# Scoring two units of a quad in one visit, with a new bank map and new planner constants, in a fused attention and gated-MLP block

## The chip, the core and the metric

The kernel runs on one core of one Trainium2 chip. The metric is device time in microseconds (us), the median of several runs; lower is better. Five engines work side by side, each with its own queue in order: TensorE (PE in the profile), VectorE (DVE), ScalarE (ACT), GpSimd (POOL) and SyncE (SP), which here issues nearly all DMAs. Data lies in SBUF; TensorE writes its products to PSUM, which has 8 banks of 128 partitions x 512 f32.

## The reference

It is one transformer block with adaptive layernorm: 2048 tokens, width 640, 32 heads of 20, MLP width 1536, in bf16.

```python
mod = (silu(c) @ w_mod).reshape(1, 6, 1, 640)      # sa, ca, ga, sb, cb, gb
h = layernorm(x) * (1 + ca) + sa
qkv = (h @ wqkv)                                   # 3 x 32 heads x 20
p = softmax(q @ k.T * 20 ** -0.5)
x = x + ga * ((p @ v) @ wo)
h = layernorm(x) * (1 + cb) + sb
x = x + gb * (((h @ w_gate) * (h @ w_up)) @ w_down)
```

There are 32 x 2048 x 2048 scores, and each needs an exponential.

## The kernel before, in words

**A planner writes the program.** `build_kernel` runs on the host. It makes a `Task` for each piece of work (engine, estimated duration, what it depends on, priority) and steps a model clock (`Sched.run`): whenever an engine is free in the model, the ready task of best priority is put next in that engine's list. The five lists are then emitted as they are, with semaphore waits for the dependencies that cross engines (`emit_program`). On the chip every engine works through its list in order, so where a task takes longer than its estimate, what stands behind it waits. PE has its own choice of the next task in `pick_pe`.

**Tiling.** Queries go in five chunks (`CHUNKS`: 512, 512, 512, 256, 256). A chunk has eight items, each one set of four heads (`items`). An item's scores are cut into units of 128 keys x 512 queries (two key tiles x 256 queries in the short chunks), 64 units an item in the long chunks. The four heads of a set lie in four groups of 32 partitions, and products of different groups run on PE at once.

**Two ways to the exponential.** Most units are scored into a group's own PSUM banks, two units at a time (even groups hold three units from group `HEADG` on), and ACT takes the exponential of a whole group in one instruction (L1444), writing the bf16 tile PP. A part of the units goes to DVE instead. `QUADS` says how many quads (four units, one for each head) of each item. DVE adds a bias to the scores, clamps at 0 and converts to int16 (L1468, 128x512, into the tile DB); the result, read as bf16 bits, is a first estimate of the power of two. Two masks (L1500 keeps the mantissa, L1508 the exponent) and one product (L1505) over the whole quad, 128x2048, then give two terms in DSS whose sum is a quadratic estimate of the exponential. The value products (PV, L1970) sum over both terms. So a unit of a quad costs one DVE read, a quarter of three wide DVE instructions, and twice the PV products.

**PE's order.** `pick_pe` first looks whether the next group's scores can be issued (a score visit). Units of quads are attached to such a visit by `d_attach`, up to two in a visit, when they come due (`due`, from `D_LEAD`), when their keys and queries are there and when one of the shared PSUM banks `G` is free. Else it takes PV products, or a round of other products (projections, the suffix), or a fill product on the identity, which is issued where the activity of the last 3.4 us in the model falls under `FILL_MIN`.

**Banks.** Before, even groups use banks 0, 1 (and 2 from `HEADG` on), odd groups 3, 4; bank 7 is for PV; the shared slots `G` are 5, 6 and 2, of which 2 is given up at `HEADG`.

**End of an item.** DVE transposes the PV sums (T1, L1592) and takes the reciprocal of the denominators (L1599); POOL multiplies (OTn, L1600); DVE transposes back (L1607); SP issues four or five small DMAs that lay the heads into Ocp (L1619). After an item 7 all of a chunk's outputs are there.

**The suffix of a chunk** (`suffix`) runs while the next chunk's scores do: the product with wo, in two halves for each tile of 128 tokens, and the residual (L1690); batch-norm statistics (L1704, L1706); variance plus epsilon, and its power -0.5 on POOL (sd L1707, rs L1709); xn, which subtracts the mean and multiplies by rs (L1711); transposes of xn on PE (L1728) and their evacuation with scale and shift (h2T, L1733); gate and up products, `hprod`, the product with wd, and the output. In chunks 0 to 2 xn stands on POOL (`XN2_POOL = 3`, with an estimate of 760 ns); in chunks 3 and 4 it stands on DVE (estimate 360 ns). With `XN2_LK = 2` the planner lets an xn on POOL start only when no ready DVE task that is marked `lk` waits, and lets neither engine start a marked task while the other runs one. The weights of gate and up come in slices (stg, L1768) by SP.

The late projections of the queries (`LATEQ`, fourth quarter of the tokens) are written to a DRAM buffer q_rows (L1177) and read back in another layout (QT, L1199), all by SP. `LATEQ_A` and `LATEQ_F` say from which group on they may run.

**The tail** is the suffix of the last chunk, which has no scores beside it.

Of the kernel before, what the change touches and what calls it, by code (L numbers as in the profile page):

```python
# [12 lines left out]
SEM = 60.0  # L13
# [14 lines left out]
STEAL_END = 66197.894  # L28
STEAL_GAP = 187.231
HAM_W = 3413.3  # L30
# [290 lines left out]
def emit_program(nc, sched, nsem_dma=56):  # L321
# [83 lines left out]
    with nc.Block() as block:  # L405
# [20 lines left out]
        def _(e):  # L426
# [6 lines left out]
         (3, 4, 3, 4, 3, 3, 4, 4),  # L433
         (3, 3, 4, 3, 3, 4, 4, 4),
         (1, 2, 1, 2, 1, 1, 1, 2),
         (1, 1, 1, 1, 1, 1, 1, 1))
D_LEAD = 0.381
NB0, NSS = 2, 3
HEADG = 579
OP_EARLY = 0  # L440
EV_OP = 0.5
T_SPLIT = 1
GU_OUTER = 4
# [6 lines left out]
XBACK = 1  # L450
HOLD = 110
PVTOL = 253
XDPRIO = 3.0
TPRIO = 0.75
# [7 lines left out]
WM_GATE = 9  # L462
WM_NEED = 1.838
K_DIRECT = (0, 1, 2, 3)
Q_DIRECT = 2
K_LEAD = 0.755
K_ALL = (0,)
KD_LEAD = 0.212
DMA_WINDOW = 900000
D_LATE = 16  # L470
D_RES = 63
PVMIN, PVMAX, PVCAP = 2, 10, 12
PV0 = 0
# [11 lines left out]
PV0N = 1  # L485
XN2_LK = 2
XN2_POOL = 3
RC_POOL = 0
RC_COST = 900
GATE_F = (0.793, 0.688, 1.105, 0.744, 1.0)  # L490
FILL_MIN = 4156.882
FILL_HARD = 0.0
# [6 lines left out]
XFIRST = 0  # L499
LN2P = 2.344  # L500
NALT = 1
OPFIRST = 0
HT_L = 0.02
V_L = 0.246
LATE_A = 3.254
LATE_L = 1.2
LATEQ = (3,)
LATEQ_A = 2
LATEQ_F = 0.578
QUAD_GAIN = 0.597233983857778  # L510
NTERM = 2
XHALF = 1
X_LATE = -0.231
X_HALF = 0.0
# [10 lines left out]
def build_kernel(nc, A_x, A_wqkv, A_wo, B_x, B_w_gate, B_w_up, B_w_down, c, w_mod, out):  # L525
# [169 lines left out]

    G = Slots([5, 6, 2] if HEADG else [5, 6], "G")
    GX = Slots([3, 4] if HEADG else [2, 3, 4], "GX")
    hx = (1, 3) if HEADG else (1, 3, 4)
# [25 lines left out]
    def pool(dur, f, deps=(), prio=3.0, **k):  # L724
        t = Task("pool", dur, f, deps, prio=prio, **k)
        t.lk = 1
        return sc.add(t)
# [63 lines left out]
    def load_rest():  # L791
# [5 lines left out]
        for q, f in enumerate((first2[0], first2[1],  # L797
# [14 lines left out]
                                               fill=1.0, base=0, channel_multiplier=1), [p_i0], prio=0)  # L812
    p_mh = pool(100, lambda e: e.memset(mhalf[:, 0:2], -0.5), prio=1)
    p_m1 = pool(100, lambda e: e.memset(mhalf[:, 2:4], -1.0), prio=2)
    p_on = dve(600, lambda e: e.memset(Vf[:, :].rearrange("p (h w) -> p h w", w=VW)[:, :, 0:1], 1.0), prio=-1)
# [463 lines left out]
    while ap < NA:  # L1279
        even = len(glist) % 2 == 0  # L1280
        us = ubuf[ap:ap + (3 if even and len(glist) >= HEADG else 2)]
        apos.append(ap)
        ap += len(us)
        glist.append((us, 0 if even else 3))
    NG = len(glist)
# [176 lines left out]
    for qi, (it, us) in enumerate(dquads):  # L1462
        st_ = d_state[qi]
        for x, u in enumerate(us):
            cell = {}

            def fp1(e, st_=st_, x=x, cell=cell):
                return e.tensor_scalar(DB0[:, st_["slot"], x * 512:(x + 1) * 512], bank(cell["b"]), EBIAS, 0.0,  # L1468
                                       op0=ALU.add, op1=ALU.max)
            tp = Task("dve", ps_cost(512), fp1, [], prio=0.8, name=f"P1.{qi}.{x}")  # L1470
            tp.on_start = lambda task, cell=cell: G.done(cell["b"], task)
            u.task = (tp, cell)
            sc.left += 1
            st_["p1"][x] = tp
# [109 lines left out]
    def item_end_tasks(it):  # L1584
# [9 lines left out]
        item_info[it]["t1"] = t1  # L1594
        den = OT[:, 0:n].rearrange("p (b c) -> p b c", c=32)[:, :, 0:1]
        if RC_POOL and it < len(items) - 1:
            t2 = pool(RC_COST, lambda e: e.tensor_tensor(invT[:, 0:nb32].unsqueeze(2), den, mhalf[:, 2:3].unsqueeze(2).to_broadcast([128, nb32, 1]), ALU.pow), [t1, p_m1], prio=0)
        else:
            t2 = dve(155, lambda e: e.reciprocal(invT[:, 0:nb32].unsqueeze(2), den), [t1], prio=1.5)  # L1599
        f3 = lambda e: e.tensor_tensor(  # L1600
# [41 lines left out]
    def suffix(ci):  # L1642
# [31 lines left out]
        for tl in range(ntl):  # L1674
# [28 lines left out]
            for hf in range(2):  # L1703
# [6 lines left out]
                      [p1], prio=1)  # L1710
            fx2 = lambda e, t=t, tl=tl: e.tensor_scalar(  # L1711
                xn2[:, tl, :], xck[:, tl, :], mv2[:, t, 0:1], rs2[:, t:t + 1], op0=ALU.subtract, op1=ALU.mult)
            if XN2_POOL and ci < XN2_POOL:
                tx = pool(760, fx2, [p2] + first, prio=1)
                tx.lk = XN2_LK
            else:
                tx = dvl(360, fx2, [p2] + first, prio=LN2T if tail else LN2P)
            t_xn2.append(tx)
            x1_done += ev
# [407 lines left out]
    def d_attach(ts, t, pos, rows, limit, relax):  # L2127
        n = 0
        while n < limit:
# [18 lines left out]
            if dst["fresh"]:  # L2148
# [5 lines left out]
                dst["fresh"] = False  # L2154
            b, rel = G.take(ga[1], 1)
            tp, cell = pick.task
            cell["b"] = b
            ts.deps = ts.deps + unit_score_deps(pick) + rel
            ts.emits = ts.emits + unit_score_emits(pick, lambda b=b: bank(b))
            tp.deps = [ts] + st_["brel"]  # L2160
# [8 lines left out]
    def pick_pe(t):  # L2169
# [44 lines left out]
        elif not tail_added[0]:  # L2214
            tail_added[0] = True
            la = [a for a in act_tasks[-2:]]
            if all(a.done is not None for a in la):
                for b in range(5):
                    if b != 2 or not HEADG or back[0]:
                        G.add(b, la)  # L2220
            else:
                tail_added[0] = False
# [143 lines left out]
```

## Time and profile before

| what | us |
|---|---|
| median of three runs | 848.92 (848.4 to 850.7) |
| the profiled execution, its own time | 848.4 |
| its span, first to last instruction | 846.8 |
| first exponential starts | 16.2 |
| last exponential ends | about 813.4 |
| ACT idle in the span | 67.6 |
| DVE idle in the span | 120.9 |
| mean granted TensorE clock | 0.972 of full speed |

The profile shows one execution. A group's row gives line, engine, operation, tiles (out<-in), shape, count, then busy time and the mean of one, then how long the engine was idle just before these instructions and what ended that. Neighbouring instructions of one engine overlap a little, so the time from start to start is below the mean of one: 14 exponentials of 1024 columns that ran without a break took 13.07 us, 0.93 each, while their mean is 1.125. A timeline line of several instructions gives their start, the time from the first's start to the last's end, and in brackets the idle time before. PE's ends are modelled, so a busy PE need not be at its peak. The granted clock says how much of full speed TensorE was given.

### The profile page before, as it was taken

The page shows a single profiled execution, that of the slowest core. Times are in us where ns is not written, and L with a number is a line of the kernel's source. Part 1 is how long each engine was busy: PE and PEld are TensorE (multiplying, and loading weights), DVE is VectorE, ACT ScalarE, POOL GpSimd, SP SyncE. Part 2 cuts the span into 40 slices and gives each one's busy share as a digit, 9 for nine tenths or more (in the row PEclk, how much of TensorE's full clock was granted, in tenths as well). Part 3 has the DMA queues.
Part 4 walks back from the last instruction along what each step waited for, and adds up shares of the span by engine and source line. Part 5 has one row for each costly group of instructions (what it writes and reads, how often), then busy time and mean ns, then how long its engine had stood idle before and what let it go on. Part 6 is the DMA issues. An engine that isn't in the chain of part 4 may idle for free.

```text
span 846.8 us, 29000 instructions
## 1 busy us (share of the span) xinstructions
PE 804.5 (95%) x12557; PEld 310.2 (37%) x12557; DVE 725.9 (86%) x1260; ACT 779.2 (92%) x821; POOL 106.8 (13%) x118
## 2 busy tenths in 40 slices
PE   9999999999796999999999799999998999999998
PEld 4433233222231223323332222334343444554567
DVE  7898999999777699999999798998987877767773
ACT  7889999999887699999999699999998999999952
POOL 3300000010015000000005300000034000001000
PEclk9999999999989599999999799999997999999999
DMA  9724211114310025200210022100300136204520
GB/s 293 218 75 100 72 43 36 44 31 123 105 36 26 24 55 154 59 7 22 60 45 6 5 56 61 37 5 29 91 9 3 39 90 122 60 23 107 129 61 23
DMA packets 116445, 54.72 MB, mean 65 GB/s; under 512 B 83915, under 2 KB 116319, under 8 KB 116319
## 3 DMA queue, kind: packets, MB, share of 16 engines
q1 hardware_dynamic: 115391, 51.72, 23.9%
q8 instruction: 100, 1.64, 0.8%
q10 hardware_dynamic: 928, 1.15, 0.4%
q14 instruction: 26, 0.21, 0.1%
HBM read 41.85 MB, written 8.41 MB: 59 GB/s over the span
## 4 chain that ended last, share of the span: by engine, by line
ACT 37%; PE 33%; DVE 15%; issue 8%; POOL 5%; DMA 1%; SPq 0%; ACTq 0%; DVEq 0%; POOLq 0%
ACT PP L1444 37%; PE ps_all L1408 10%; PE ps_all L871 9%; PE ps_all L1970 7%; DVE DB L1468 6%; POOL xn L1711 4%; PE ps_all L867 3%; DVE DSS L1505 2%; DVE DSS L1508 2%; DVE DSS L1500 1%; PE ps_all L1131 1%; PE ps_all L1067 1%; PE ps_all L1728 1%; DMA wm<-in_w_mod_dram 1%; DVE OT L1592 1%
## 5 line engine op out<-in xcount | busy, mean ns | idle before, releaser
L1444 ACT ACTIVATE PP<-ps_all 128x1024 bf16<-128x1024 f32 (+1 forms) x777 | 760.2, 1178 | 33.5 <-PE ps_all L1408 31.4
L1408 PE MATMUL ps_all<-QT,KT 32*128 32x512 bf16 (+1 forms) x2560 | 314.6, 346 | 16.1 <-ACT PP L1444 12.1
L1468 DVE TENSOR_SCALAR DB<-ps_all 128x512 int16<-128x512 f32 x396 | 263.0, 681 | 50.6 <-PE ps_all L1408 49.3
L1408 PEld LDWEIGHTS ps_all<-QT,KT 32*128 32x128 bf16 x2560 | 82.2, 91 | 268.0 <-ACT PP L1444 232.5
L1970 PE MATMUL ps_all<-PP,Vf 128*32 128x512 bf16 (+2 forms) x2088 | 167.9, 349 | 0.3 <-DVE OT L1592 0.2
L871 PE MATMUL ps_all<-h2T,stg 128*32 128x512 bf16 (+1 forms) x1780 | 119.8, 347 | 1.1 <-DVE DB L1468 0.4
L1505 DVE TENSOR_TENSOR DSS<-DB,DSS 128x2048 bf16<-128x2048 bf16 x99 | 120.8, 1220 | 0.0
L1600 POOL TENSOR_TENSOR OTn<-OT,invT 128x512 bf16<-128x512 f32 (+1 forms) x39 | 42.8, 1096 | 600.0 <-DVE invT L1599 596.2
L1970 PEld LDWEIGHTS ps_all<-PP,Vf 128*32 128x32 bf16 (+1 forms) x2088 | 46.7, 94 | 91.9 <-issue 84.5
L1970 PE MATMUL ps_all<-DSS,Vf 128*32 128x512 bf16 (+3 forms) x944 | 78.9, 357 | 0.7 <-DVE DSS L1508 0.5
L1500 DVE TENSOR_SCALAR DSS<-DB 128x2048 int16<-128x2048 int16 x99 | 72.2, 730 | 1.0
L1508 DVE TENSOR_SCALAR DSS<-DB 128x2048 int16<-128x2048 int16 x99 | 69.3, 700 | 0.0
L871 PE MATMUL ps_all<-wd,hprod 128*32 128x320 bf16 (+1 forms) x1320 | 57.6, 283 | 1.1 <-DVE DB L1468 0.8
L871 PEld LDWEIGHTS ps_all<-h2T,stg 128*32 128x32 bf16 x1780 | 39.7, 96 | 36.7 <-issue 18.8
L871 PEld LDWEIGHTS ps_all<-wd,hprod 128*32 128x32 bf16 x1320 | 30.7, 96 | 18.1 <-issue 8.3
L1592 DVE STREAM_TRANSPOSE OT<-ps_all 128x512 f32<-128x512 f32 (+1 forms) x40 | 24.1, 603 | 13.6 <-PE ps_all L1970 13.5
L1711 POOL TENSOR_SCALAR xn<-xck,mv,rs 128x640 bf16<-128x640 bf16 x12 | 32.2, 2689 | 12.0 <-DVE DSS L1505 11.5
L871 PE MATMUL ps_all<-wo,Ocp 128*32 128x320 bf16 (+1 forms) x640 | 29.0, 291 | 4.1 <-DMA Ocp<-OcT 3.9
L1970 PEld LDWEIGHTS ps_all<-DSS,Vf 128*32 128x32 bf16 (+1 forms) x944 | 24.1, 96 | 22.4 <-issue 10.9
L1131 PE MATMUL ps_all<-hT,wq 128*32 128x512 bf16 x375 | 31.9, 382 | 0.0
L2290 PE MATMUL ps_all<-ident 128*32 128x512 bf16 x352 | 30.9, 386 | 0.4
L871 PE MATMUL ps_all<-wV,hT 128*32 128x320 bf16 (+1 forms) x688 | 31.1, 291 | 0.0
(123 smaller groups left out, 542.3 us busy)
## 6 DMA issues: line engine op xcount, KB each, us to landing
stg<-in_B_w_gate_dram SPq DMA_DIRECT2D x50, 160.0 KB
stg<-in_B_w_up_dram SPq DMA_DIRECT2D x50, 160.0 KB
QT<-q_rows SPq DMA_DIRECT2D x22, 128.0 KB
KT<-k_rows SPq DMA_DIRECT2D x84, 32.0 KB
wm<-in_w_mod_dram SPq DMA_DIRECT2D x3, 800.0 KB
x<-in_A_x_dram SPq DMA_DIRECT2D x7, 320.0 KB
xck<-in_A_x_dram SPq DMA_DIRECT2D x3, 640.0 KB
wd<-in_B_w_down_dram SPq DMA_DIRECT2D x1, 1920.0 KB
```

What stands on the lines that cost most here:

```text
L871: return lambda e, b: e.matmul(ps[32 * x:32 * x + 32, b, c0 + o:c0 + o + w], lhs()[:, 32 * x:32 * x + 32], rhs() if w == n else rhs()[:, o ...
L1131: f = [lambda e, b_, k=k, x=x: e.matmul(ps[x:x + min(32, w - x), b_, :], wx[:, k, r0 + x:r0 + min(x + 32, w)], hT[tc][:, k, :], tile_posit ...
L1408: ems.append(lambda e, i=i, kt=kt: e.matmul(dstf()[:, i * u.n:(i + 1) * u.n], KT[32 * u.s:32 * u.s + 32, u.j, kt * 128:(kt + 1) * 128], QT ...
L1444: return e.activation(PPs[g % 2][:, cellp["p"], 0:nu * 512], ps[:, b0:b0 + nu, :].rearrange("p b c -> p (b c)"), AFT.Exp, scale=ESCALE)
L1468: return e.tensor_scalar(DB0[:, st_["slot"], x * 512:(x + 1) * 512], bank(cell["b"]), EBIAS, 0.0, op0=ALU.add, op1=ALU.max)
L1500: return e.tensor_scalar(DSS[:, st_["ss"][0], :], DB0[:, st_["slot"], :], 0x7F, 0x3F00, op0=ALU.bitwise_and, op1=ALU.bitwise_or)
L1505: return e.tensor_tensor(d, DB0[:, st_["slot"], :].bitcast(BF16), d, ALU.mult)
L1508: return e.tensor_scalar(DSS[:, st_["ss"][1], :], DB0[:, st_["slot"], :], 0x7F80, 2, op0=ALU.bitwise_and, op1=ALU.bitwise_or)
L1592: t1 = Task("dve", n * 1.1 + 70, lambda e: e.transpose(OT[:, 0:n], ps[:, BPV, 0:n]), [], prio=0.0, name=f"T1.{it}")
L1600: f3 = lambda e: e.tensor_tensor(OTn[:, 0:n].rearrange("p (b c) -> p b c", c=32), OT[:, 0:n].rearrange("p (b c) -> p b c", c=32), invT[:, ...
L1711: fx2 = lambda e, t=t, tl=tl: e.tensor_scalar(xn2[:, tl, :], xck[:, tl, :], mv2[:, t, 0:1], rs2[:, t:t + 1], op0=ALU.subtract, op1=ALU.mult)
L1970: ems.append(lambda e, i=i, kt=kt, stt=stt, stp=stp: e.matmul(ps[32 * s:32 * s + mc, BPV, 0:u.n], Vf[:, (kt * H + 4 * u.j + s) * VW:(kt * ...
```

## The change

It does five things.

1. `xn` of chunks 0 to 2 goes back from POOL to DVE, as in chunks 3 and 4; the options for it, and the unused option to take the reciprocal on POOL, are removed.
2. Bank map: odd groups use banks 5, 6; the shared slots are 4, 3 and 2, so that two of them are neighbours (3 and 4, or 2 and 3).
3. Pairs: `d_attach` looks, for each unit that it attaches, for a second unit of the same quad that is also ready. Where banks 3 and 4 (or 2 and 3) are both free and the second unit is due as well, both are scored in this visit, and one DVE instruction of 128x1024 reads both banks and writes both places of DB. It is estimated at 1120 ns, a single one at 600.
4. `QUADS`: chunk 2's quads are arranged differently; the last chunk has 9 in place of 8, so there are 100 quads in place of 99.
5. Constants: lead times, gates, priorities, fill limits, and in the tail `T_SPLIT` 0 (transposes of the last xn evacuated 256 wide, not 128) and `OP_EARLY` 1 (the product with wo begins before the last item is done, and only its last part waits).

```diff
-STEAL_GAP = 187.231
+STEAL_GAP = 115.475
...
-         (3, 3, 4, 3, 3, 4, 4, 4),
+         (3, 3, 4, 4, 3, 4, 4, 3),
          (1, 2, 1, 2, 1, 1, 1, 2),
-         (1, 1, 1, 1, 1, 1, 1, 1))
-D_LEAD = 0.381
+         (2, 1, 1, 1, 0, 2, 1, 1))
+D_LEAD = 0.34
...
-HEADG = 579
-OP_EARLY = 0
+HEADG = 580
+OP_EARLY = 1
-T_SPLIT = 1
+T_SPLIT = 0
...
-D_RES = 63
-PVMIN, PVMAX, PVCAP = 2, 10, 12
+D_RES = 114
+PVMIN, PVMAX, PVCAP = 4, 14, 10
...
-XN2_LK = 2
-XN2_POOL = 3
-RC_POOL = 0
-RC_COST = 900
-GATE_F = (0.793, 0.688, 1.105, 0.744, 1.0)
-FILL_MIN = 4156.882
+P1_PAIR = 1
+P1_PCOST = 1120.0
+GATE_F = (0.91, 0.621, 0.409, 0.425, 1.0)
+FILL_MIN = 4121.401
...
-LATE_A = 3.254
-LATE_L = 1.2
+LATE_A = 3.033
+LATE_L = 3.352
 LATEQ = (3,)
-LATEQ_A = 2
-LATEQ_F = 0.578
+LATEQ_A = 19
+LATEQ_F = 0.632
...
-    G = Slots([5, 6, 2] if HEADG else [5, 6], "G")
-    GX = Slots([3, 4] if HEADG else [2, 3, 4], "GX")
+    G = Slots([4, 3, 2], "G")
+    GX = Slots([5, 6], "GX")
...
-        glist.append((us, 0 if even else 3))
+        glist.append((us, 0 if even else 5))
...
             def fp1(e, st_=st_, x=x, cell=cell):
+                if len(cell["bs"]) == 2:
+                    (ba, bb), (xa, xb) = cell["bs"], cell["xs"]
+                    return e.tensor_scalar(
+                        DB0[:, st_["slot"], :].rearrange("p (x c) -> p x c", c=512)[:, xa:xb + 1:xb - xa, :],
+                        ps[:, ba:bb + 1:bb - ba, :], EBIAS, 0.0, op0=ALU.add, op1=ALU.max)
...
-            if XN2_POOL and ci < XN2_POOL:
-                tx = pool(760, fx2, [p2] + first, prio=1)
-                tx.lk = XN2_LK
-            else:
-                tx = dvl(360, fx2, [p2] + first, prio=LN2T if tail else LN2P)
-            t_xn2.append(tx)
+            t_xn2.append(dvl(360, lambda e, t=t, tl=tl: e.tensor_scalar(
+                xn2[:, tl, :], xck[:, tl, :], mv2[:, t, 0:1], rs2[:, t:t + 1], op0=ALU.subtract, op1=ALU.mult),
+                [p2] + first, prio=LN2T if tail else LN2P))
...
+            if P1_PAIR and limit - n >= 2:
+                for u in dst["left"]:
+                    if u is not pick and (u.s not in rows or relax) and all(
+                            d.done is not None and d.done + SEM <= t for d in unit_score_deps(u)):
+                        mate = u
+                        break
+                av = [i_ for i_, r_ in G.free if all(z.done + SEM <= t for z in r_)]
+                two_ = next(((i_, i_ + 1) for i_ in (3, 2) if i_ in av and i_ + 1 in av), None)
+                if two_ is None:
+                    mate = None
+                if mate is not None and due[dst["next"] + 1] > pos:
+                    mate = None
...
+                tp.dur = P1_PCOST
```

## The prediction

> **What bounds the kernel now.** I read the page's busy shares first, then the waits, then tables of busy time over chosen stretches, then the timeline of the stretches that stood out, and last the groups kept apart by form.
>
> ```profile
> PE 804.5 (95%) x12557; PEld 310.2 (37%) x12557; DVE 725.9 (86%) x1260; ACT 779.2 (92%) x821; POOL 106.8 (13%) x118
> ...
> ACT PP L1444 <- PE ps_all L1408: 31.4, 31, 6.8
> ...
> PE ps_all L1728 <- POOL xn L1711: 12.2, 3, 6.8
> ...
> PE ps_all L871 <- DMA Ocp<-OcT: 3.9, 1, 3.9
> ```
>
> The first line is the page's part 1; the others are waits (who waited for whom, us in total, times, longest). ScalarE (ACT) is nearly full, so the time is its busy time plus its idle time, 846.8 - 779.2 = 67.6 us. Of this, 45.45 us busy in the first 57 us leaves 11.6 us at the head, and 6.44 busy in the last 32.9 us leaves 26.5 us for the tail; some 29 us lie between. There ACT waits for scores (L1408), and TensorE, which issues in a fixed order, is late with scores when an earlier instruction in its order waits: transposes (L1728) for GpSimd's xn (L1711), once a product (L871) for a DMA. Busy time by stretch (columns: stretch, length, then PE, PEld, DVE, ACT and POOL busy with counts, granted clock, DMA share, GB/s):
>
> ```profile
> 218.60:422.10 203.50, 188.85 (x2621) 60.19 (x2613) 180.96 (x291) 185.82 (x202) 25.67 (x20) 0.93 0.21 53
> 422.10:613.90 191.80, 181.77 (x2540) 59.05 (x2540) 174.85 (x275) 184.96 (x196) 27.28 (x20) 0.97 0.15 37
> 613.90:813.90 200.00, 190.16 (x4074) 93.39 (x4075) 152.11 (x277) 196.11 (x173) 26.93 (x33) 0.97 0.30 67
> ...
> 228.00:242.00 14.00, 10.12 (x142) 3.38 (x146) 7.46 (x14) 8.38 (x9) 0.65 (x2) 0.76 0.31 72
> 268.00:294.00 26.00, 19.20 (x158) 5.13 (x154) 13.56 (x22) 14.27 (x15) 9.31 (x5) 0.61 0.08 20
> 466.00:480.00 14.00, 9.19 (x69) 3.09 (x65) 8.00 (x14) 7.41 (x8) 7.12 (x3) 0.65 0.00 0
> 642.00:660.00 18.00, 15.90 (x224) 6.37 (x228) 12.33 (x24) 14.63 (x14) 3.79 (x4) 0.72 0.05 12
> ...
> 300.00:420.00 120.00, 117.95 (x1785) 39.16 (x1777) 118.72 (x188) 119.69 (x132) 7.60 (x5) 1.00 0.24 61
> ```
>
> The first three stretches run between output transposes, about query chunks 1, 2 and 3 to 4. Nearly all idle time of ACT in the middle stands in four short stretches: 14.00 - 8.38 = 5.62, 26.00 - 14.27 = 11.73, 14.00 - 7.41 = 6.59 and 18.00 - 14.63 = 3.37, together 27.3 us, and these are where the granted clock is 0.61 to 0.76. In the last line ACT idles 0.31 us of 120 though VectorE (DVE) is busy for 118.72: a full DVE alone does not stop ACT here. The timeline of the second, for POOL and ACT:
>
> ```profile
> 265.84 10.42 POOL L1711 TENSOR_SCALAR xn<-xck,mv,rs 128x640 bf16<-128x640 bf16 x4 [6.54 <-DVE DSS L1505]
> ...
> 277.36 1.02 ACT L1444 ACTIVATE PP<-ps_all 128x1024 bf16<-128x1024 f32 x1 [6.76 <-PE ps_all L1408]
> ```
>
> Four xn in a row take 10.42 us, 2.6 each, against the 760 ns that the planner counts; the transposes stand in PE's order for the earlier end, PE waits, then runs at a low clock, and ACT starves during both.
>
> **The change part by part.** Prices come from these rows (mean ns of one is after the bar):
>
> ```profile
> L1444 ACT ACTIVATE PP<-ps_all 128x1024 bf16<-128x1024 f32 x679 | 647.5, 1125 | 30.5 <-PE ps_all L1408 28.4 <-PE ps_all L1970 1.4
> L1468 DVE TENSOR_SCALAR DB<-ps_all 128x512 int16<-128x512 f32 x396 | 263.0, 681 | 50.6 <-PE ps_all L1408 49.3
> ...
> L1711 POOL TENSOR_SCALAR xn<-xck,mv,rs 128x640 bf16<-128x640 bf16 x12 | 32.2, 2689 | 12.0 <-DVE DSS L1505 11.5
> ...
> L1711 DVE TENSOR_SCALAR xn2t<-xckt,mv,rs 128x640 bf16<-128x640 bf16 x2 | 0.9, 446 | 0.3 <-POOL rs L1709 0.2
> ```
>
> *xn of chunks 0 to 2 leaves GpSimd.* The built order of the new program has no xn on POOL and twelve more on DVE, each waiting for POOL's rs. If the transposes then never wait, ACT gets back 11.73 + 6.59 + 3.37 = 21.7 us. The third stretch also holds a wait of PE for DVE DB (0.76 us beside 0.63 for xn), so I take half of it: 11.73 + 6.59 + 1.7 = 20.0. Lower end: only the 12.2 us that PE is shown waiting for xn.
>
> *It arrives on DVE.* Rows overlap by about 0.08 us (four L1468 in 2.48 us, so 0.60 from start to start, against 0.68 each), so an xn costs 0.446 - 0.08 = 0.37, and twelve 4.4 us, 1.5 in each chunk. Chunk 1 is the tightest: 180.96 + 1.5 = 182.5 us of DVE under ACT's 185.82. That cover of 3.3 us hides it; without it 1.5 us a chunk is paid. The new wait: behind an xn in DVE's order stand L1468 reads, batch-norm statistics and quad terms, and for them wait score visits, which need the banks. POOL's rs took 0.56 us alone and 1.61 beside DVE work, so an xn may hold DVE up to 1.0 us, 12 in all; before the four xn that DVE already does it was idle 0.3 us in all. Between 0 and 4.4 + 12 = 16.4 I take 2.5, near the low end, because the rows that do the same thing (xn2t, above) lie there.
>
> *The DMA stall at 228 us.* Before, SP had three weight loads, one Ocp, two q_rows writes and then three Ocp; the transpose feeding them ended at 222.6, the last issue at 231.3, and PE went on at 232.5, 1.25 after. In the new order the late Q rounds begin 17 groups later, the six weight loads stand ahead of all four Ocp and no q_rows write stands between. The loads wait for no compute, so I expect SP to be through with them. Four issues at 0.77 from 222.6, and 1.25 to land, is 226.9. PE now opens the wo product after 9 score visits behind the item's last PV product, not 11, two visits of 0.91 us earlier: 228.64 - 1.8 = 226.8. A wait near 0.1 remains. Of 5.6 us I take 4.5; ends: 5.6, and -1.8 if SP is as late as before.
>
> *ACT loses two exponentials* (679 to 677 of 1024 columns; one quad more goes to DVE in chunk 4): two in a row take 1.81, so 1.8 us.
>
> *That quad* costs DVE four L1468 at 0.60, two masks (L1500, L1508) at 0.60 and a product at 1.13, 4.7 us, in a stretch where it is busy for 152 of 200 us. At nothing; 0 to 4.7.
>
> *Pairs.* The built order has 25 instructions of 128x1024 and 350 of 128x512 in place of 396. No row has 1024 columns on DVE. The PSUM reads of 512, 320 and 256 columns take 681, 483 and 420 ns: 1.02 ns a column and 159 fixed, so 1.20 us, 1.12 start to start, against two at 0.60. That saves 0.08 each, 2.0 us of DVE in all; ends 0 and 25 x 0.23 (no start-up at all) = 5.8. DVE is not what ends the wait, so nothing on the path. The price is that a pair waits for both scores and holds two of the three shared banks; with 25 pairs among 375 reads I take nothing, from -1 to +3.
>
> *Fill products* drop from 352 to 284: PE gets idle, not ACT. *Tail:* after the last score PE is busy without a gap from 812 us; the new order splits the transposes less and opens the wo product before the last PV product, but PE's products there are nearly the same set. 0, within 1 either way. *Head and all other constants* reorder everything; I take 0, within 2.5, as the stretches without a stall show ACT full already.
>
> *Sum*, against the profiled execution's 848.4 us (span 846.8 and 1.6 around it): 848.4 - 20.0 + 2.5 - 4.5 - 1.8 = 824.6. The median of the runs, 848.92, is 0.5 higher, so 825.1, forecast 825.
>
> *A rule weighed.* At 647.8 us a score visit goes from 0.41 to 0.61 us after PE gaps of only 0.52, 0.35, 0.63 and 0.76 us in the 10 us before; so here short gaps go with a clock loss that cost up to 3.37 us of ACT. The Trainium skill, "TensorE: Matmul & The Clock Gate", section "Why this matters for your kernels", asks for no idle gap above about 3 us between bursts, so that by it short waits are free and an xn held up on DVE would cost its own length alone; that rule would put the time at the low end of my range. The row decides, and I keep a rival for it.
>
> **The rivals.**
> *A: VectorE becomes the bound* (chance 0.16). For: 182.5 of 185.8 in chunk 1. If every xn waits 1.0 us for rs, a chunk has four more us and 1.3 us of idle per 120 as in the 300 to 420 row (2.0 per chunk): 182.5 + 4 + 2 = 188.5, 2.7 over ACT; chunk 2, 176.4 + 5.9 = 182.3, stays under 184.96. With two short clock losses at 3.37 it gives 825 + 2.7 + 6.7 = 834. Against: 300 to 420.
> *B: the DMA wait stays* (0.12). For: PE comes 1.8 us earlier and six loads of about 0.5 us stand in front. 825 + 4.5 + 1.8 = 831.
> *C: slower, by the clock* (0.06). Place: the suffix of every chunk, where xn, rs and the transposes now form one chain over DVE and POOL, with 68 fewer fills to bridge gaps. Price: 3.4 to 6.6 us of ACT for each loss of clock, as in the stretches of 642 and 466. The gain of 24 us is gone after five at 5.0; six or seven give 825 + 30 = 855. Against: outside the four stretches the clock reads 1.00.
> *D: it doesn't do what it says* (0.06): the transposes are late again for another reason, only the 12.2 us come back, with the DMA wait kept: 825 + 7.8 + 4.5 = 837.
>
> **How the numbers follow.** The forecast has 0.60 and its own range 819 to 830: 825 - 1.7 (the third stretch) - 1.1 (DMA) - 2.5 (DVE) - 1 is about 819, and 5 us above for head and reordering. The range to hold 8 in 10 reaches to A and B: 818 to 834; C, D and part of A are left out. A measurement of this kernel tells from no change what is over 0.3%, 2.5 us. All but C are below 846: faster 0.93, same 0.01, slower 0.06.
>
> **What would show it.** Right: no wait of L1723 (the transposes) for POOL, the ACT wait for scores down from 31.4 to under 10 us, clock about 1.0 through the middle, DVE near 732, ACT near 776. The pair row shows 1.15 to 1.25 us. Wrong: clock below 0.8 in any slice, a wait of DVE xn for POOL rs above 5 us in total, PE waiting for Ocp.

## The result, and the profile after

The changed kernel takes 826.84 us (median of six runs, 825.72 to 829.87), the kernel before 848.66 beside it: a ratio of 0.9752, 95% interval 0.9721 to 0.9783. The profiled execution of the changed kernel took 825.72 us, with a span of 823.9. The first lines are busy times by engine (page, part 1), the second who waited for whom, with us in total, times and the longest.

```profile
PE 790.0 (96%) x12485; PEld 307.1 (37%) x12485; DVE 727.3 (88%) x1252; ACT 773.9 (94%) x816; POOL 70.4 (9%) x105
```

```profile
ACT PP L1441 <- PE ps_all L1405: 9.3, 15, 2.5
...
PE ps_all L1405 <- issue: 2.9, 1, 2.9
```

ScalarE waits 9.3 us for scores instead of 31.4, and its idle time falls from 67.6 to 823.9 - 773.9 = 50.0 us. No wait of the transposes for xn is left, and none of TensorE for Ocp. Line numbers have moved by up to five: scores are L1405, exponentials L1441, transposes L1723, and the single and the paired reads L1470 and L1467. Next, busy time by stretch (length, then PE, PEld, DVE, ACT, POOL with counts, granted clock, DMA share, GB/s); the cut between the first two rows is the end of the last exponential, and the last four rows are the times of the four stalls of before.

```profile
57.00:789.75 732.75, 704.89 (x11247) 257.85 (x11243) 663.19 (x1080) 722.32 (x739) 54.98 (x68) 1.00 0.24 57
789.75:823.90 34.15, 31.21 (x420) 24.46 (x417) 16.85 (x44) 5.49 (x14) 1.29 (x2) 1.00 0.10 29
228.00:242.00 14.00, 13.61 (x201) 4.54 (x197) 11.42 (x23) 14.00 (x17) 0.79 (x2) 1.00 0.03 8
268.00:294.00 26.00, 25.81 (x351) 7.83 (x355) 25.43 (x41) 26.00 (x29) 1.37 (x1) 1.00 0.23 57
466.00:480.00 14.00, 13.92 (x196) 4.03 (x189) 13.75 (x20) 14.00 (x17) 0.00 (x0) 1.00 0.30 68
642.00:660.00 18.00, 17.41 (x368) 7.85 (x360) 15.54 (x27) 18.00 (x17) 1.23 (x2) 1.00 0.22 49
```

The same cut for the kernel before:

```profile
57.00:813.40 756.40, 719.56 (x11334) 260.61 (x11328) 660.14 (x1084) 727.28 (x742) 91.36 (x80) 0.97 0.23 55
813.40:846.80 33.40, 30.45 (x390) 24.08 (x382) 16.55 (x44) 6.44 (x17) 1.23 (x2) 1.00 0.06 21
```

Between 57 us and the last exponential, ScalarE idles 732.75 - 722.32 = 10.43 us instead of 29.12, and its busy time there falls by 4.96; the tail grows from 33.40 to 34.15. So the span's 22.9 us are 18.69 + 4.96 - 0.75. The four stalls gave 27.31; 8.62 of that were lost again elsewhere. The largest new loss stands at 89 us (timeline: start, us, engine, what; in brackets the idle time before):

```profile
76.62 9.49 SPq L1187 DMA_DIRECT2D KT<-k_rows  x16
86.24 1.64 SPq L1174 DMA_DIRECT2D q_rows<-KPA  x3
88.00 2.22 SPq L1619 DMA_DIRECT2D Ocp<-OcT  x3
90.33 0.87 SPq L1196 DMA_DIRECT2D QT<-q_rows  x2
...
92.41 0.39 PE L1405 MATMUL ps_all<-QT,KT 32*128 32x512 bf16 x3 [2.87 <-issue]
```

TensorE stands still for 2.87 us before a score visit, and SP issues two QT loads 2 us before it goes on. From 80 to 100 us ScalarE idles 3.64. The groups of the moved and the new operation:

```profile
L1467 DVE TENSOR_SCALAR DB<-ps_all 128x1024 int16<-128x1024 f32 x25 | 30.4, 1214 | 0.2 <-PE ps_all L1405 0.2
...
L1711 DVE TENSOR_SCALAR xn<-xck,mv,rs 128x640 bf16<-128x640 bf16 x12 | 5.1, 434 | 0.1
```

### The profile page after: what moved, and what is told of

Same layout as the page of the kernel before. It is cut to its first block, busy times and chain, and to the rows that moved or that the text cites. A ratio compares the mean times of both kernels' runs of the same rounds, so it can differ in the third digit from the quotient of the medians.

```text
span 823.9 us, 28833 instructions
## 1 busy us (share of the span) xinstructions
PE 790.0 (96%) x12485; PEld 307.1 (37%) x12485; DVE 727.3 (88%) x1252; ACT 773.9 (94%) x816; POOL 70.4 (9%) x105
## 4 chain that ended last, share of the span: by engine, by line
ACT 46%; PE 37%; issue 10%; DVE 5%; DMA 1%; ACTq 0%; DVEq 0%
ACT PP L1441 46%; PE ps_all L868 12%; PE ps_all L1405 11%; PE ps_all L1965 8%; PE ps_all L864 3%; DVE DB L1470 1%; PE ps_all L1128 1%; PE ps_all L1064 1%; DMA wm<-in_w_mod_dram 1%; DVE DSS L1511 1%; PE ps_all L1025 1%; DVE DSS L1503 1%; DVE DSS L1508 1%; DVE DB L1467 0%; PE ps_all L2326 0%
## 5 line engine op out<-in xcount | busy, mean ns | idle before, releaser
L1441 ACT ACTIVATE PP<-ps_all 128x1024 bf16<-128x1024 f32 (+1 forms) x775 | 755.9, 1218 | 14.0 <-PE ps_all L1405 9.3
L1405 PE MATMUL ps_all<-QT,KT 32*128 32x512 bf16 (+1 forms) x2560 | 311.1, 340 | 23.0 <-ACT PP L1441 17.6
L1470 DVE TENSOR_SCALAR DB<-ps_all 128x512 int16<-128x512 f32 x350 | 234.7, 683 | 43.9 <-PE ps_all L1405 43.1
L1405 PEld LDWEIGHTS ps_all<-QT,KT 32*128 32x128 bf16 x2560 | 82.5, 91 | 270.7 <-ACT PP L1441 240.9
L1965 PE MATMUL ps_all<-PP,Vf 128*32 128x512 bf16 (+2 forms) x2080 | 164.4, 344 | 0.2 <-DVE OT L1595 0.2
L1508 DVE TENSOR_TENSOR DSS<-DB,DSS 128x2048 bf16<-128x2048 bf16 x100 | 121.7, 1217 | 0.0
L1965 PE MATMUL ps_all<-DSS,Vf 128*32 128x512 bf16 (+1 forms) x960 | 79.2, 351 | 1.5 <-DVE DSS L1511 1.4
L1503 DVE TENSOR_SCALAR DSS<-DB 128x2048 int16<-128x2048 int16 x100 | 68.9, 689 | 1.2
L1511 DVE TENSOR_SCALAR DSS<-DB 128x2048 int16<-128x2048 int16 x100 | 69.7, 697 | 0.0
L868 PE MATMUL ps_all<-wd,hprod 128*32 128x320 bf16 (+1 forms) x1320 | 60.3, 284 | 0.0
L1965 PEld LDWEIGHTS ps_all<-DSS,Vf 128*32 128x32 bf16 x960 | 24.3, 95 | 24.0 <-issue 9.7
L1467 DVE TENSOR_SCALAR DB<-ps_all 128x1024 int16<-128x1024 f32 x25 | 30.4, 1214 | 0.2 <-PE ps_all L1405 0.2
L1823 DVE TENSOR_TENSOR hprod<-ps_all,gsb 128x512 bf16<-128x512 f32 x36 | 24.6, 683 | 2.4 <-PE ps_all L868 2.4
```

Of the source, the lines that this page charges most:

```text
L868: return lambda e, b: e.matmul(ps[32 * x:32 * x + 32, b, c0 + o:c0 + o + w], lhs()[:, 32 * x:32 * x + 32], rhs() if w == n else rhs()[:, o ...
L1405: ems.append(lambda e, i=i, kt=kt: e.matmul(dstf()[:, i * u.n:(i + 1) * u.n], KT[32 * u.s:32 * u.s + 32, u.j, kt * 128:(kt + 1) * 128], QT ...
L1441: return e.activation(PPs[g % 2][:, cellp["p"], 0:nu * 512], ps[:, b0:b0 + nu, :].rearrange("p b c -> p (b c)"), AFT.Exp, scale=ESCALE)
L1467: return e.tensor_scalar(DB0[:, st_["slot"], :].rearrange("p (x c) -> p x c", c=512)[:, xa:xb + 1:xb - xa, :], ps[:, ba:bb + 1:bb - ba, :] ...
L1503: return e.tensor_scalar(DSS[:, st_["ss"][0], :], DB0[:, st_["slot"], :], 0x7F, 0x3F00, op0=ALU.bitwise_and, op1=ALU.bitwise_or)
L1508: return e.tensor_tensor(d, DB0[:, st_["slot"], :].bitcast(BF16), d, ALU.mult)
```

## The experiments

All kernels are planned anew by the program itself, so one constant can move work far behind its own place. To keep apart what an edit does and what the new plan does elsewhere, each profile is cut at the end of the last exponential. "Left" counts the gate and up products of chunk 3 (h2Tt by stg, some 500 in all) that stand behind the last score visit in TensorE's order. Each ratio is against runs of the kernel before that were made beside that kernel's own (their medians are 847.46 to 849.08), and it is not exactly the quotient of two medians.

| kernel | median us | ratio to before, 95% interval | last exponential ends | tail | left |
|---|---|---|---|---|---|
| before | 848.66 | 1 | 813.4 | 33.4 | 0 |
| changed | 826.84 | 0.9752 (0.9721 to 0.9783) | 789.8 | 34.2 | 12 |
| e1: before, xn on VectorE | 832.90 | 0.9829 (0.9792 to 0.9865) | 793.7 | 38.3 | 120 |
| e2: changed, no pairs | 825.16 | 0.9749 (0.9722 to 0.9775) | 786.8 | 35.8 | 40 |
| e3: before, xn counted 2600 ns | 847.05 | 1.0000 (0.9977 to 1.0023) | 794.2 | 49.5 | 360 |
| e4: changed, xn on GpSimd | 855.45 | 1.0105 (1.0079 to 1.0130) | 813.0 | 40.0 | 160 |
| e5: e1 and LATEQ_A 19 | 828.70 | 0.9764 (0.9732 to 0.9795) | 792.2 | 35.5 | 40 |
| e6: changed, LATEQ_A 2 | 839.31 | 0.9887 (0.9852 to 0.9923) | 797.9 | 41.9 | 204 |
| e8: changed, chunk 3 planned late | 849.16 | 1.0004 (0.9982 to 1.0026) | 800.5 | 47.5 | 360 |
| e9: changed, q_rows writes first | 828.90 | 0.9763 (0.9738 to 0.9787) | 787.9 | 39.8 | 92 |
| e10: e1 and LATE_L 3.352 | 821.21 | 0.9692 (0.9664 to 0.9719) | 783.9 | 35.5 | 40 |
| e11: e10 and HOLD 119 | 820.80 | 0.9696 (0.9661 to 0.9731) | 785.6 | 33.6 | 0 |
| e12: e3 without the lock rule | 835.26 | 0.9861 (0.9834 to 0.9888) | 798.1 | 36.0 | 40 |
| e13: changed, K_LEAD 0.9 | 823.16 | 0.9712 (0.9680 to 0.9744) | 790.1 | 33.9 | 12 |

**e1: xn alone.**

```diff
-XN2_POOL = 3
+XN2_POOL = 0
```

> The kernel before with one constant changed, so that the twelve xn of chunks 0 to 2 are planned and run on VectorE; no pairs, all other constants as before. Theory (slow xn on GpSimd make the transposes late, and TensorE and ScalarE pay for it): the three stretches of 268, 466 and 642 us lose their idle time, 21.7 us of ScalarE, against up to 2.5 for the work on VectorE: 827 to 832 us, with the DMA wait at 228 us (5.6 us of ScalarE idle) still there, since the order up to that point is unchanged. No wait of the transposes for xn. Rival (the gain comes mostly from the other constants and the pairs, which shape the whole order): the time stays above 838 us, and new idle stretches of ScalarE open elsewhere. Rival (VectorE becomes the bound): 835 or more, with ScalarE waiting while VectorE is busy all the time in chunk 1.

It took 832.9, just above the theory's range. Its stretches, the last two cut at the last exponential:

```profile
220.00:240.00 20.00, 15.93 (x181) 4.49 (x181) 11.93 (x18) 14.14 (x16) 0.98 (x1) 0.83 0.41 101
...
57.00:793.70 736.70, 711.09 (x11194) 256.40 (x11190) 660.05 (x1090) 725.75 (x743) 56.20 (x68) 0.99 0.23 55
793.70:832.00 38.30, 34.16 (x522) 27.19 (x510) 18.34 (x49) 6.80 (x18) 1.09 (x2) 1.00 0.18 44
```

The stall of the Ocp copies is still there (20.00 - 14.14 = 5.86 us of ScalarE), the three xn stalls are gone, and the last exponential ends 19.7 us earlier. But the tail grew by 4.9 us, which the theory did not have: 108 gate and up products of chunk 3 (3.7 us of TensorE) lie behind the last exponential, and none did before.

**e2: no pairs.**

```diff
-P1_PAIR = 1
+P1_PAIR = 0
```

> The changed kernel with the pairs switched off and nothing else touched: every score unit of the quads is read by its own VectorE instruction of 128x512. Theory (pairs save VectorE some 2 us in all and VectorE does not end the waits): the time is within 2.5 us of the changed kernel's 826.8, and VectorE's busy time is about 2 us above 727.3. Rival (the pairs carry part of the gain, because VectorE is the tightest in chunk 1): 4 to 12 us slower than the changed kernel, with score visits of TensorE waiting for the VectorE reads DB. Rival (a pair holds two of three shared banks and costs more than it saves): 2 to 6 us faster than the changed kernel.

825.2 us; the intervals of the two ratios (0.9722 to 0.9775 and 0.9721 to 0.9783) nearly coincide. The reads take 266.2 us of VectorE in 400 singles, and 234.7 + 30.4 = 265.1 with pairs, so the pairs save about 1.1 us of it, and the time shows no use of that. The gain does not need the feature that gives the change its name. What the pairs do by themselves e2 does not tell, since the plan moved too: without them SP issues the two QT loads at 87.28 instead of 90.33 and ScalarE does not idle from 80 to 100 us, while the tail is 1.6 us longer.

**e3: the estimate corrected, xn left on GpSimd.**

```diff
-                tx = pool(760, fx2, [p2] + first, prio=1)
+                tx = pool(2600, fx2, [p2] + first, prio=1)
```

> The kernel before with the twelve xn left on GpSimd, but counted by the planner at 2600 ns, as the trace shows them, in place of 760. GpSimd's work is the same; only the places of the transposes and of what follows them in each engine's order move. Theory (the loss is the late transposes, not GpSimd's work): the waits of the transposes for xn vanish and the time is 827 to 835 us although GpSimd is as busy as before. Rival (a chain of four xn in a row is too slow in itself: the wait moves to the products that follow, or weights and banks are held longer): 838 to 850 us.

The theory fell: 847.05, no change. The stalls by xn did vanish, and the last exponential ends at 794.2, as early as in e1; but the tail takes 49.5 us. The timeline of GpSimd for chunk 2, and from the groups of the tail the products left:

```profile
641.28 2.52 POOL L1711 TENSOR_SCALAR xn<-xck,mv,rs 128x640 bf16<-128x640 bf16 x1 [1.27 <-DVE DSS L1505]
...
649.77 2.52 POOL L1711 TENSOR_SCALAR xn<-xck,mv,rs 128x640 bf16<-128x640 bf16 x1 [2.97 <-DVE DSS L1505]
...
656.20 2.52 POOL L1711 TENSOR_SCALAR xn<-xck,mv,rs 128x640 bf16<-128x640 bf16 x1 [1.74 <-DVE DSS L1505]
...
661.53 2.51 POOL L1711 TENSOR_SCALAR xn<-xck,mv,rs 128x640 bf16<-128x640 bf16 x1 [1.79 <-DVE DSS L1505]
```

```profile
L871 PE MATMUL ps_all<-h2Tt,stg 128*32 128x256 bf16 x360 | 11.9, 274 | 3.5 <-DMA stg<-in_B_w_up_dram 3.5
```

The four xn take from 641.28 to 664.04, 22.8 us for 10.1 us of work (14.0 in the kernel before), since each waits until a VectorE quad instruction is through, 7.8 us in all, and other work of GpSimd comes between. Chunk 2's transposes come 20 us later than in the kernel before, chunk 3's transposes start only 13 us before the last exponential (39 before), and 360 of its products are done after it, with 3.5 us of waits for their weights.

**e4: xn put back on GpSimd in the changed kernel**, at 760 ns and with the lock rule, as before.

```diff
-            t_xn2.append(dvl(360, lambda e, t=t, tl=tl: e.tensor_scalar(
+            if ci < 3:
+                tx = pool(760, fx2, [p2] + first, prio=1)
+                tx.lk = 2
```

> The changed kernel with the twelve xn of chunks 0 to 2 put back on GpSimd at the old estimate of 760 ns; pairs and all other constants as changed. Theory: the price of the misplaced xn does not depend on the other constants, so the three stalls come back, 12 to 22 us of waits and lost clock: 839 to 849 us. Rival (the new constants leave slack that hides late xn, so that they are a cause of the gain of their own): 826 to 833 us.

855.45, 6 us beyond the theory. Between 57 us and the last exponential ScalarE idles 755.97 - 724.56 = 31.4 us, 21.0 more than in the changed kernel; that is the price foreseen. The tail is 5.9 longer, with 160 products left. The new constants hide nothing of a late xn:

```profile
L1728 PE MATMUL ps_all<-ident,xn 128*128 128x128 bf16 x60 | 9.0, 294 | 9.4 <-POOL xn L1711 8.6 <-DVE DB L1470 0.8
```

**e5: xn and the late Q rounds.**

```diff
-LATEQ_A = 2
+LATEQ_A = 19
-XN2_POOL = 3
+XN2_POOL = 0
```

> The kernel before with two constants changed: the twelve xn on VectorE, and the late Q rounds of the last key tile 17 groups later (LATEQ_A 19 for 2); no pairs. Its last score comes with 40 products of chunk 3 (h2Tt by weights) still behind it in TensorE's order, where the run with xn alone has 120 and the kernel before none. Theory (the DMA stall at 228 us comes from Q work ahead of the transposes and of the Ocp copies; the rest of the loss of the xn run was those products behind the last score, about 0.034 us each by 3.7 us for 108): ScalarE's last exponential ends at 788 us, 5.6 earlier than with xn alone, the tail is 36 us instead of 38.3, together 824 to 827 us: these two constants are then the whole gain, and the pairs and the other thirty constants add nothing. Rival (the DMA stall has another cause): 829 to 833 us, with ScalarE idle for 4 us or more between 220 and 240. Rival (the other constants are a cause of their own): 829 or more without that stall.

828.7. The tail came out as expected (35.5), the stall did not go: 5.48 us of idle time between 220 and 240. Timeline of SP, and of TensorE:

```profile
221.30 1.31 SPq L1177 DMA_DIRECT2D q_rows<-KPA  x2
224.66 0.81 SPq L1199 DMA_DIRECT2D QT<-q_rows  x2
...
227.12 3.05 SPq L1619 DMA_DIRECT2D Ocp<-OcT  x4
```

```profile
231.42 0.46 PE L871 MATMUL ps_all<-wo,Ocp 128*32 128x320 bf16 x4 [3.23 <-DMA Ocp<-OcT]
```

SP issues nothing from 222.6 to 224.66: at the head of its queue stand two QT loads that read what the two q_rows writes before them have just sent off. The waits of SP name such a wait, here for the whole of the kernel before:

```profile
SPq L1199 <- DMA q_rows<-KPA: 4.0, 4, 1.6
```

The Ocp copies, whose OcT was written at 222.8, come behind these and three weight loads. Of the 4.3 us until the first copy the pause is 1.9, the two QT loads 0.8 and the weight loads 1.6. These are Q projections of the ordinary tiles, not the late ones.

**e6: the late Q rounds early again in the changed kernel.**

```diff
-LATEQ_A = 19
+LATEQ_A = 2
```

> The changed kernel with the late Q rounds put back to the early place (LATEQ_A 2 for 19); pairs and all else as changed. 204 products of chunk 3 stand behind the last score, 12 in the changed kernel; the two q_rows writes stand ahead of the Ocp copies again, behind six weight loads. Theory (DMA stall and tail, each by its own cause): the stall near 225 us is back with 2 to 5.6 us of ScalarE idle time, and the tail grows by 192 products at 0.034 = 6.5 us: 835 to 839 us. Rival (no DMA stall, the tail alone): 833. Rival (neither matters): 826 to 828.

839.3, just above the theory's range but not for its reason: there is no stall between 220 and 240. The tail grew by 7.7 us (204 left), and the other 8.1 us opened at places that no theory named, the largest 3.2 us of ScalarE between 680 and 700 at a clock of 0.75. By itself LATEQ_A neither makes nor ends the Ocp stall.

**e8: chunk 3 planned late in the changed kernel.**

```diff
-            t_xn2.append(dvl(360, lambda e, t=t, tl=tl: e.tensor_scalar(
+            t_xn2.append(dvl(10360 if ci == NC - 2 else 360, lambda e, t=t, tl=tl: e.tensor_scalar(
```

> The changed kernel with one number changed: the planner counts each of the two xn of chunk 3 at 10360 ns instead of 360, so that the transposes of chunk 3 and the products behind them stand later in TensorE's order; the instructions are the same but for fills, and the order is the same up to there. 360 products of chunk 3 stand behind the last score instead of 12. Theory (the tail is set by how much of chunk 3 is left behind the last score): ScalarE's last exponential ends where it does in the changed kernel, at 789 to 790 us, and the tail grows from 34.2 to 46 us or more, 348 products at 0.034 us, with up to 3.5 more for weights that arrive late: 838 to 843 us. Rival (the tail is a chain of chunk 4's own steps, and the left products fit between them): 826 to 831 us.

The tail is 47.5 us, as the theory had it; the rival is out. But the time is 849.2: the last exponential ended 10.7 us later too, with one wait of 8.55 at 774 to 782 us, in a stretch at half clock that the last section shows. TensorE waits there five times for VectorE's quad work, 0.51 to 0.72 us each, so the clock need not be the whole reason; this was not taken apart.

**e9: q_rows writes ahead of KT loads in the changed kernel.**

```diff
-..., [te], prio=1.5, dur=450.0)
+..., [te], prio=1.3 if kind == "Q" and tc == 0 else 1.5, dur=450.0)
```

> The changed kernel with one priority changed: the q_rows writes of the first key tile are issued by SP ahead of KT loads (priority 1.3 instead of 1.5), so that near 85 us the order is 5 KT loads, the three q_rows writes, 11 KT loads, two QT loads and then the Ocp copies; before, the writes stood behind all 16 KT loads, and the QT loads behind three Ocp copies. 92 products of chunk 3 stand behind the last score, 12 in the changed kernel. Theory (TensorE's 2.9 us at 89 us wait for the QT loads, late because of SP's queue): that wait is gone, ScalarE's last exponential ends at 786 to 787 us, the tail is 2.7 us longer, 825 to 827 in all. Rival (TensorE waits there for something else, such as its own instructions): the idle time of 3.6 us between 80 and 100 stays, and the time is 829 to 831.

828.9, between the two. SP issued the QT loads at 89.06 instead of 90.33, TensorE went on at 91.68 instead of 92.41, and this time the profile names what it waits for:

```profile
PE ps_all L1405 <- DMA QT<-q_rows: 2.1, 1, 2.1
```

So the wait is for QT, and it was only shortened, since 11 KT loads still stood ahead. The tail took the rest: 39.8 us.

**e10 and e11: the stall at its cause, and the tail.** e10 is e1 with the first of these two edits, e11 is e1 with both. Both values are those of the changed kernel. HOLD says how many ns ahead of a score visit the planner gives TensorE at most half of a round of other products.

```diff
-LATE_L = 1.2
+LATE_L = 3.352
-HOLD = 110
+HOLD = 119
```

> The kernel before with the twelve xn on VectorE and LATE_L 3.352 for 1.2, which starts the projections of the later key tiles up to two item lengths earlier; LATEQ_A stays at 2. The traces of the two runs whose stall stayed show SP held at 222 to 224 us by two QT loads that wait for q_rows writes, with the weight loads and the Ocp copies behind them; here those QT loads stand ahead of four of the last Ocp copies of the item before. 40 products of chunk 3 stand behind the last score (120 with xn alone). Theory (the DMA stall is SP's queue, held by late Q work of the ordinary tiles): no idle stretch between 220 and 240, ScalarE's last exponential at 788 to 789 us (793.7 with xn alone), tail 36 us, 824 to 827 us. Rival (the stall has another cause): 829 to 833, with 4 us or more of idle time between 220 and 240.

> As the run with xn on VectorE and LATE_L 3.352, and HOLD 119 for 110: three constants of the kernel before, no pairs. No product of chunk 3 stands behind the last score. Theory (what is left behind the last score sets the tail): ScalarE's last exponential within 1.5 us of that of the run without HOLD, the tail shorter by 1.4 us or more (40 products at 0.034) and near 34: 822 to 825 us. Rival (the tail does not follow that count): the time of the run without HOLD, within 1 us.

e10 took 821.2, 3 us below the theory's range. Its SP, and the product that waited 3.88 us before:

```profile
210.84 1.26 SPq L1177 DMA_DIRECT2D q_rows<-KPA  x2
...
214.75 0.89 SPq L1199 DMA_DIRECT2D QT<-q_rows  x2
...
225.20 0.76 SPq L1619 DMA_DIRECT2D Ocp<-OcT  x1
...
227.00 2.27 SPq L1619 DMA_DIRECT2D Ocp<-OcT  x3
```

```profile
230.95 0.31 PE L871 MATMUL ps_all<-wo,Ocp 128*32 128x320 bf16 x4
```

The QT loads are through 10 us earlier, SP is free when OcT is ready (225.17), and TensorE doesn't wait. The last exponential ends 9.8 us earlier than in e1, more than the 5.9 of the stall; small idle stretches behind it went as well. LATE_L moved the q_rows writes, the QT loads and the weight loads together, so e10 shows that the Q rounds of the ordinary tiles set the stall; it does not divide it between the pause and the loads behind it. e11 took 820.8: the tail shrank by 1.9 us as the count says, and the last exponential came 1.7 later, 0.2 beyond the bound that was set. But its time lies below the theory's range and within 1 us of e10, as the rival had it: what the tail gave, the last exponential took. e10 beats the changed kernel (its interval ends at 0.9719, the changed kernel's begins at 0.9721), and both its edits are parts of the change. So everything else in the change, pairs, bank map, quads and the other constants, costs about 0.6% when put on top of these two.

**e12: GpSimd without the lock rule.** e3 with

```diff
-XN2_LK = 2
+XN2_LK = 0
```

> The kernel before with the twelve xn still on GpSimd, counted at 2600 ns, and with the planner's rule switched off that keeps such an xn apart from VectorE's two-byte instructions (XN2_LK 0 for 2). In the run with 2600 ns alone each xn waited for a VectorE DSS instruction by that rule, and the four of chunk 2 took 22.8 us; 360 products of chunk 3 stood behind the last score, and here 40. Theory (what the xn cost on GpSimd is their place in the plan: too early and TensorE waits, too late and the tail grows; their 2.5 us each cost nothing): no stalls by xn, ScalarE's last exponential near 794 us with the DMA stall of 228 us still there, tail 36 us, 829 to 834 us. Rival (GpSimd and VectorE hold each other up when they run together): VectorE's rows grow by a tenth or more (L1505 above 1.35 us, L1468 above 0.75), and the time is 838 us or more.

835.3, 1 us above the theory's range and clearly below the rival's, with all twelve xn on GpSimd. The means of VectorE's rows did not grow (L1505 1217 ns after 1220, L1468 682 after 681), but they could hardly show it: only 16 of the 297 quad instructions ran beside an xn. The most that was seen among these is an L1500 of 1.24 us, 0.55 above the row's median of 0.68; one L1505 took 1.53. The xn rows grew, from 2689 to 2861 ns:

```profile
440.15 6.05 POOL L1711 TENSOR_SCALAR xn<-xck,mv,rs 128x640 bf16<-128x640 bf16 x2
...
448.19 3.90 POOL L1711 TENSOR_SCALAR xn<-xck,mv,rs 128x640 bf16<-128x640 bf16 x1
```

This last one took 1.4 us longer than one alone (2.50). It began while an L1508 ran (447.97 to 448.65), and an L1505, which was not lengthened, followed at once until 449.79. TensorE waited for xn again, 1.9 us. ScalarE idles 1.6 us at 260 to 280 and 5.7 at 440 to 480, where e1 has none. The Trainium skill ("SBUF — State Buffer", section "Who interferes with whom") says that the later of two such instructions on VectorE and GpSimd is blocked outright for the whole of the other; this xn, which came second, fits that, and so does the L1500 of 1.24 us, which began 0.7 us before an xn ended. The planner's rule holds in its model only: in the kernel before, with the rule on, one xn took 4.18 us beside an L1508 and an L1505.

**e13: K_LEAD in the changed kernel.**

```diff
-K_LEAD = 0.693
+K_LEAD = 0.9
```

> The changed kernel with K_LEAD 0.9 for 0.693, which plans the K and Q rounds of the first item some 5 us earlier; SP issues the QT loads ahead of the Ocp copies and two of the three q_rows writes behind 8 KT loads instead of 16. 12 products of chunk 3 stand behind the last score, as in the changed kernel. Theory (TensorE's wait at 89 us is for the QT loads): it is gone, with the 3.6 us of ScalarE between 80 and 100, and nothing else moves: ScalarE's last exponential at 786 us, tail 34, 822 to 824.5 us. Rival (the wait moves to the next load in SP's queue): 825 to 828 us, with ScalarE idle as long at another place before 200 us.

823.2. The idle time between 80 and 100 is gone (QT loads at 84.32, ahead of all Ocp copies). But idle time opened at another place, as the rival said:

```profile
140.00:160.00 20.00, 18.91 (x257) 7.40 (x254) 15.51 (x25) 15.61 (x17) 0.31 (x1) 0.91 0.13 39
```

4.39 us of idle ScalarE at 140 to 160, where the changed kernel has 1.19. It did not come by the rival's way, for TensorE waits for no load there: it waits for ScalarE twice, 0.53 us each, at 148.8 and 149.7, then has half its clock for 3.4 us from 150.0 and makes no score visit until 153.8. The profiled execution took 825.8; whether the other five, down to 821.0, have this stall is open.

## Why the prediction was right, and where it was not

Forecast and result lie within 2 us, and the main step holds. Not all steps do.

**What bounds it**: right. In every kernel here the time is the end of the last exponential plus the tail, and the first moves with ScalarE's idle time.

**xn leaves GpSimd (20.0) and arrives on VectorE (2.5)**: the first right, the second too dear. By e1 the last exponential ends 19.7 us earlier with both effects in it. The twelve xn cost 5.1 us of VectorE (434 ns each), which nothing waited for, and the idle time before them is 0.1 us: the wait for rs did not come. What the step lacked is the tail. By itself the move gained 1.71% of 848.7, 14.5 us, since the plan left 120 products behind the last score.

The reason given, that the transposes were planned for the wrong time, holds for the stalls and not for the whole gain. e3 planned them for the right time: the stalls went and the last exponential came 19 us earlier, but nothing was gained, as the lock rule then spread the four xn over 22.8 us and the tail grew. e12 dropped that rule too and gained 1.39%, 11.8 of e1's 14.5 us, with all xn on GpSimd. The 2.7 us between them are not clear of noise, as the two intervals overlap, and they set two tails against each other: e12's last exponential comes 4.4 us after e1's, and its tail is 2.3 shorter, with 40 products left instead of 120. So at most a few us are the price of xn's speed there; the rest was its place in the plan, too early or too late.

**The DMA stall (4.5)**: the size nearly right, the cause right in part only, and given back. The prediction blamed the late Q rounds (LATEQ_A) and counted the weight loads and q_rows writes ahead of the Ocp copies. e5 and e6 show that LATEQ_A by itself neither removes nor restores the stall; e10 shows what does remove it: LATE_L, which moves the QT loads and what stands behind them out of the way. The weight loads had a share, 1.6 us in e5. That two loads at the head of SP's queue were waiting themselves could be read in the trace of before, in a pause of SP from 222.4 to 224.4, and was overlooked. And while 5.62 us came back, in the changed kernel ScalarE idles 3.64 us around 89 us, where TensorE waits for other QT loads in the same queue (e9, e13): net 2.0.

**ACT's two exponentials (1.8)**: ScalarE's busy time before the last exponential fell by 4.96, of which 0.67 had merely moved into the first 57 us. Most of the rest above 1.8 goes with the waits: between 57 us and the last exponential an exponential of 1024 columns adds 1.02 us to the busy time when it follows a wait and 0.92 when it follows another without a break, and 36 followed a wait before, 16 in the changed kernel. Twenty at 0.1 are 2 us, so a wait of ScalarE costs a little more than its idle time.

**The quad, the pairs and the fills (0)**: right for the pairs, by e2. The pair's row reads 1.214 us, 1.20 was worked out. The quad and the fills were not tried alone.

**Tail (0, within 1)**: 0.75, right for this kernel, wrong as a rule. The prediction took it as a fixed set of products. It holds only where the products of chunk 3 are done in time, and in the twelve experiments it ran from 33.6 to 49.5.

**Head and all other constants (0, within 2.5)**: besides the QT wait, 10.43 - 3.64 = 6.8 us of middle idle time where the kernel before had 29.12 - 27.31 = 1.8. That is 5.0 lost, twice the bound; the 4.96 of ScalarE's busy time hid it in the sum. So the closeness of the sum is in part luck. Measured on the span, xn (21.7, and nothing for VectorE) and ScalarE's busy time gave 7.4 us more than was set, and the DMA term, the tail and the other constants gave 8.3 less.

**The rivals.** A did not come: DVE's 727.3 us end no wait of note. B came in another place, for 3.6 us where 6.3 were set. C did not come in the changed kernel. That the clock can be lost without a long wait e8 shows, but not at C's place: it fell at 754.7 us, after TensorE had waited for ScalarE six times within 8 us. D did not come.

**The rule weighed.** After the gap of 2.87 us at 89 us the changed kernel's clock reads 0.68 and 0.56 for 4.6 us, so the clock was lost after a gap of less than 3 us, and e8 lost it with none above 0.95. The row of before, not the 3 us of the Trainium skill's page, was the right guide.

## What to carry to other kernels

Cut each profile at the end of the bound engine's last work: a retuned schedule can win 20 us ahead of the cut and lose 16 behind it, and only the cut shows both. Where a planner writes the order, a wrong estimate shows as a wait, but putting it right need not pay: see which other rule then binds, and count what the new order leaves for the end. Before you blame the transfers that stand ahead of a late one, look for a pause in the queue itself, since a load that waits for an earlier write holds all that follow.

## What the hardware showed unexpectedly

The granted clock fell without any long gap. In e8 (stretches as above) TensorE's longest gap from 744 to 755 us is 0.95:

```profile
748.00:752.00 4.00, 3.07 (x56) 1.03 (x48) 0.00 (x0) 4.00 (x5) 0.00 (x0) 1.00 0.69 170
752.00:756.00 4.00, 2.85 (x38) 1.06 (x38) 0.33 (x1) 4.00 (x4) 0.00 (x0) 0.84 1.22 231
756.00:760.00 4.00, 3.62 (x40) 1.21 (x39) 2.86 (x8) 3.83 (x5) 1.40 (x3) 0.50 0.51 98
...
776.00:780.00 4.00, 1.85 (x16) 0.42 (x16) 3.97 (x5) 0.00 (x0) 0.00 (x0) 0.50 0.00 0
```

It then stayed at 0.50 until 785.5; in 28 us of that, 756 to 784, TensorE was busy 21.64. In the kernel before it stayed there though TensorE showed no gap at all (its ends are modelled, so short pauses may be hidden):

```profile
280.00:284.00 4.00, 4.00 (x31) 1.49 (x27) 2.54 (x7) 2.92 (x3) 1.05 (x1) 0.50 0.00 0
284.00:288.00 4.00, 4.00 (x40) 0.85 (x36) 3.01 (x5) 2.41 (x3) 0.00 (x0) 0.50 0.02 4
288.00:292.00 4.00, 4.00 (x35) 0.74 (x27) 1.63 (x3) 2.60 (x3) 0.00 (x0) 0.50 0.08 21
```

After the gap at 89 us it was back within 5 us. What sets the return was not tried. In all fourteen traces the clock is either 1.00 or 0.50, and the stretches at 0.50 within the kernels last 3.4, 6.8, 10.2, 13.7, 20.5 and 30.7 us, all multiples of 3.4; values between are means over a window. And SP took 0.59 us for each of the sixteen KT loads at 76.62 (9.49 in all; 0.44 to 0.66 in rows of eight), so that everything behind them was held for nearly ten.
